# Spectral mixer with gMLP gate: w_in tail rows loaded as four 32-row transfers, and a reordered start of the chunk schedule

## The chip, the cores and the metric

The kernel runs on one core of one Trainium2 chip. The metric is the device time in microseconds of one execution. The engines are named as the profile names them: PE (TensorE, matrix products), PEld (its weight loads), DVE (VectorE), ACT (ScalarE), POOL (GpSimd) and SP (SyncE, which only issues DMA transfers here). "SPq", "ACTq" and "POOLq" are the issue of transfers on those queues.

## The reference

The input x is 2048 rows of 576 values in bf16. After a layer norm, the result goes two ways, and both are joined at the end.

```
xn = layernorm(A_x)                                  # (1, 2048, 576)

# branch A: a filter in the frequency domain
X  = rfft2(xn); X = X * (w_r + 1j * w_i)             # (2048, 289) complex
s  = irfft2(X)                                       # (2048, 576)

# branch B: a gated MLP with a product over the sequence
z  = gelu(xn @ w_in)                                 # w_in: (576, 4608)
z1 = z[..., :2304];  z2 = layernorm(z[..., 2304:])
g  = einsum('ts,bsf->btf', w_sp, z2) + b_sp          # w_sp: (2048, 2048)
b  = (z1 * g) @ w_out                                # w_out: (2304, 576)

return A_x + s * silu(b)
```

The inputs A_x, w_r, w_i, w_in, w_sp, b_sp and w_out are bf16. B_x is not used.

## The kernel before, in words

The 2048 rows are 16 tiles of 128 rows, counted by m. Four tiles of x are one group in SBUF (`XC[0]` to `XC[3]`).

**Start and row DFT.** For each tile m, `ln1` takes the row statistics on DVE (two L259 instructions and L260), and the reciprocal root comes from ACT (L263) for m below 2 and from POOL (L248, L250) for the others. `ln1_apply` (L276, L279) writes the normalised tile to one of three buffers. It splits the 576 columns into two halves of 288, each with 256 main columns and 32 "tail" columns, so a tile has five blocks of 128: four main ones and one that holds both halves' tails, twice. `xpose` (L287) transposes the five blocks on PE into one PSUM buffer, and ACT copies them to `xnT` (L288). `p0_fold` (L294, L295, DVE) forms sums and differences of the halves, and `p0` (L302, six products of 290 columns) is the DFT along a row, with the constants CDSD. ACT copies it out (L304), and POOL stores it to DRAM (L306).

**Chunks.** The product with w_in is cut into 168 chunks: 96 "z2" chunks (one row tile by 384 columns, L410) and 72 "z1" chunks (128 columns by 512 rows, L495). A chunk has four products over 128 rows of w_in and one over the 64 tail rows (two halves of 32). The tail rows lie twice in SBUF, in partitions 0 to 63 and 64 to 127, so that two tail products of different chunks run beside each other. `fill(n)` emits the next n chunks in the order of the string `kinds`; with every fourth chunk it emits the tails of four chunks, of which two are held open in PSUM. ACT applies gelu (L429, L423, L504). For z2, DVE takes statistics (L437) and normalises in place (L466). These DVE steps are queued, and each chunk emits up to `pace` of them. The chunks are put between the steps of the DFT as filling, so that PE has work while the DFT waits.

**Order.** SP, PE and DVE run in the order in which the program is written. The order on ACT and POOL is set by the scheduler. The stages are: the loop over m with row DFTs and chunks; eleven chunks; `p1` (L320), the first column DFT; twelve chunks; `p2` and `p3` (L344, L356), the second column DFT, the filter and its inverse; twelve chunks; `p4` (L370) and `p5` (L385), the inverse transforms, whose result is stored as Yd; the remaining chunks; then the product with w_sp (`main`, L558) and the output product (`outm`, L612). Between the DFT stages the data go through DRAM and back. The transposed blocks of w_sp ("slabs") are loaded by L476, and `slab_sums` (L481) forms sums of them, because the 2x2 block product is done with seven block products instead of eight.

**Loads.** All loads of the start are on SP's queue, in this order: tiles 0 and 1 of x, CDSD, tiles 2 and 3, then three times the group of four transfers of `load_win` for 768 columns of w_in followed by four tiles of x (L223), then constants G1 (L244). `load_win` has two transfers for the main rows (L231) and two for the tails (L233); each of the two tail transfers reads 2 x 32 rows and fills 64 partitions:

```
for r in range(2):
    nc.sync.dma_start(out=t[r * KT:(r + 1) * KT, KS - 1, :], in_=wv[:, 2 * P:H2, fs])
```

Here `wv` is w_in seen as two halves, so the source is [2, 32, columns]. The same function later loads six groups of 384 columns for the z1 chunks.

PSUM has two pools of buffers: "h" with four buffers, for transposes and chunks, and "a" with two, for the DFT steps. At the very start, PE runs ten products on zeros (L673), and two more after the first transpose (L677).

Of the kernel before, what the change touches and what calls it, by code (L numbers as in the profile page):

```python
# [14 lines left out]
P = 128  # L15
# [71 lines left out]
def kernel(  # L87
# [59 lines left out]
    nc.scalar.dma_start(out=ident[:], in_=cd_id.ap())  # L147
# [66 lines left out]

    def load_x(c):
        t = AIN[c][:, 0:4 * D].rearrange("p (m d) -> p m d", m=4)
        if c == 0:
            for i in range(4):
                nc.sync.dma_start(out=t[:, i, :], in_=xv[:, i, :])
                if i == 1:  # L220
                    nc.sync.dma_start(out=CDSD, in_=cd_cdsd.ap().rearrange("p (a k l) -> p a k l", a=2, k=3))
        else:
            nc.sync.dma_start(out=t, in_=xv[:, 4 * c:4 * c + 4, :])  # L223
        return t
# [4 lines left out]
    def load_win(t, fs):  # L229
        for a in range(2):  # L230
            nc.sync.dma_start(out=t[:, a:KS - 1:2, :], in_=wv[a, 0:2 * P, fs].rearrange("(b p) f -> p b f", p=P))  # L231
        for r in range(2):
            nc.sync.dma_start(out=t[r * KT:(r + 1) * KT, KS - 1, :], in_=wv[:, 2 * P:H2, fs])  # L233
# [6 lines left out]
    XC = [load_x(0)]  # L240
    for g in range(3):
        load_win(WIN2[:, :, 2 * g * ZC:2 * (g + 1) * ZC], slice(Fh + 2 * g * ZC, Fh + 2 * (g + 1) * ZC))
        XC.append(load_x(g + 1))
# [9 lines left out]
    def ln1(ms):  # L253
        n = len(ms)
        mv = small.tile([P, n, 2], F32, tag=f"mv{n}", bufs=5)
        for i, m in enumerate(ms):
            st = small.tile([P, 2, 6], F32, tag="st1", bufs=4)
            for h in range(2):
                nc.vector.bn_stats(out=st[:, h, :], in_=XC[m // 4][:, m % 4, h * H2:(h + 1) * H2])  # L259
            nc.vector.bn_aggr(out=mv[:, i, :], in_=st[:])  # L260
        if ms[0] < 2:
            rs = small.tile([P, n], F32, tag=f"l1{n}r", bufs=5)
            nc.scalar.activation(out=rs[:], in_=mv[:, :, 1], func=ACT.Sqrt, bias=eps[:], scale=1.0)  # L263
            nc.vector.reciprocal(out=rs[:], in_=rs[:])
        else:
            rs = rstd_of(mv, n, f"l1{n}")
        for i, m in enumerate(ms):
            ln1_of[m] = (mv[:, i, 0:1], rs[:, i:i + 1])

    ln1_of = {}  # L270
# [200 lines left out]
    SA = dict(P1=4, P2=1, P5=2, P4=3, P6=0, P7=5, P3=6)  # L471
# [6 lines left out]
    def slab_sums(i, it):  # L478
        for o, a, b, op in ((5, 4, 2, ALU.subtract), (2, 2, 3, ALU.add), (0, 2, 4, ALU.subtract), (6, 1, 0, ALU.subtract)):
# [152 lines left out]
    kinds = "2" * (MT + 12) + "2221" * 4 + "2" * 12 + "12112111" * 6 + "21" * 12 + "2212" * 3 + "22112221"  # L632
# [11 lines left out]
    def fill(n, pace=1):  # L644
        for _ in range(n):
# [5 lines left out]
            if i % 4 == 1:  # L651
                done = held[:]
# [16 lines left out]
    with tc.manual_schedule(engines={SP, PE, DVE}):  # L669
# [9 lines left out]
        ln1([0])  # L679
        ln1_apply(0)  # L680
        xpose(0)
        keep_warm(2)
        ln1([1])
        ln1_apply(1)
        nc.scalar.activation(out=THF[:, 0:1], in_=ln1_of[1][0], func=ACT.Gelu_apprx_tanh)
        p0_fold(0)
        xpose(1)
        ln1([2])
        p0(0)
        fill(1, 0)  # L690
        ln1_apply(2)
        p0_fold(1)
        fill(1, 0)
        xpose(2)
        p0(1)
        ln1([3])
        ln1_apply(3)
        fill(1, 0)
        nc.sync.dma_start(out=MM, in_=cd_mm.ap().rearrange("p (a k) -> p a k", a=3))
        ln1([4])  # L700
        for m in range(2, MT):
# [3 lines left out]
            if m + 3 < MT:  # L705
                ln1([m + 3])
# [3 lines left out]
            p0(m)  # L710
            if m in (6, 9):
# [5 lines left out]
        for s2 in range(0, N2, 2):  # L717
            p1(s2)
            fill(1)
# [17 lines left out]
        for u in range(4 * NLC):  # L737
            p4(u)
            fill(1)
# [6 lines left out]
        rest = kinds.rindex("2") + 1 - place[0]  # L746
        for i in range(NT // P):
            fill(rest // 4, 2)
            slab_sums(i, 0)
# [54 lines left out]
```

## Time and profile before

| | before |
|---|---|
| median of 11 runs | 519.28 us (516.62 to 524.11) |
| profiled execution: time, span | 519.93 us, 518.1 us |
| PE busy, share of the span | 503.6 us, 97% |
| DVE, ACT, POOL busy | 332.8, 171.6, 208.1 us |
| mean granted clock of PE | 0.986 |
| HBM read, written | 40.55 MB, 21.26 MB |
| chunks done when the loop over m ends (51.28 us) | 17 of 168 |

The span runs from the first to the last instruction; the time of the execution is 1.8 us longer. The profile cuts the span into 40 slices (of 13 us), and gives for each the busy share in tenths, the clock that PE was granted, and how busy the 16 DMA engines were. Stretches of any length can be asked for in the same way. A line of the timeline gives start, length, engine, source line, operation, and in brackets the idle time before it and what ended it. Line numbers are those of the kernel before; the changed kernel's own lines differ by a few.

### The profile page before, as it was taken

What the parts mean: (1) busy time and instruction counts of PE and PEld (TensorE: products, weight loads), DVE (VectorE), ACT (ScalarE), POOL (GpSimd) and SP (SyncE); (2) the same over time, 40 slices, a digit from 0 to 9 for tenths busy, and PEclk for the clock granted to TensorE, in tenths of its full rate; (3) what the DMA queues carried; (4) which work ended last, traced back from release to release, by engine and by line L of the source; (5) the groups of instructions that cost most, each with busy time, mean ns of one, the idle gap of its engine ahead of it and who ended that gap; (6) DMA issues with size and microseconds to landing.
All of it is one profiled execution on the core that took longest, in us unless ns stands there. A gap on an engine that the chain in (4) does not pass through costs nothing.

```text
span 518.1 us, 9262 instructions
## 1 busy us (share of the span) xinstructions
PE 503.6 (97%) x3454; PEld 316.6 (61%) x3454; DVE 332.8 (64%) x712; ACT 171.6 (33%) x356; POOL 208.1 (40%) x285
## 2 busy tenths in 40 slices
PE   6979999999999999999999999999999999999996
PEld 2546554444546664356666577666666678888885
DVE  5676989655536484956656656766666637777734
ACT  4666878656557857520000001100000011000001
POOL 2455133523332486854344411344434301555500
PEclk9798999999999999999999999999999999999999
DMA  8673768887566696464021269412111655111302
GB/s 252 175 245 103 241 224 254 276 260 231 166 194 232 136 242 173 142 193 147 31 62 32 62 128 211 131 43 61 31 51 42 148 103 149 33 42 42 86 17 77
DMA packets 85409, 70.81 MB, mean 137 GB/s; under 512 B 39220, under 2 KB 77876, under 8 KB 85108
## 3 DMA queue, kind: packets, MB, share of 16 engines
q1 hardware_dynamic: 80068, 56.08, 40.6%
q0 software_dynamic: 5152, 14.11, 8.3%
q8 instruction: 27, 0.44, 0.4%
q14 instruction: 18, 0.15, 0.1%
q10 hardware_dynamic: 144, 0.03, 0.0%
HBM read 40.55 MB, written 21.26 MB: 119 GB/s over the span
## 4 chain that ended last, share of the span: by engine, by line
PE 86%; SPq 6%; DMA 5%; DVE 1%; issue 1%; ACT 1%; POOL 0%; DVEq 0%; POOLq 0%
PE pm L558 42%; PE ph L495 14%; PE ph L410 13%; PE po L612 9%; DMA AR<-in_A_x_dram 3%; SPq L476 2%; PE pa L385 2%; PE pb L356 2%; SPq L233 1%; PE pa L370 1%; DMA AR<-c_cdsd 1%; PE pa L320 1%; PE pa L302 1%; PE pa L344 1%; PE pl L612 1%; SPq L231 1%
## 5 line engine op out<-in xcount | busy, mean ns | idle before, releaser
L558 PE MATMUL pm<-AR,Z 128*128 128x384 bf16 (+1 forms) x864 | 138.8, 308 | 0.0
L562 DVE TENSOR_TENSOR AR<-pm,AR 128x384 f32<-128x384 f32 (+3 forms) x162 | 82.1, 512 | 71.8 <-PE pm L558 39.7
L558 PEld LDWEIGHTS <-Z 128*128 128x128 bf16 x864 | 84.5, 98 | 40.6
L558 PE MATMUL pm<-AR 128*128 128x384 bf16 (+1 forms) x648 | 107.0, 308 | 1.2 <-DVE AR L481 0.9
L410 PE MATMUL ph<-AR 128*128 128x384 bf16 (+1 forms) x480 | 92.5, 334 | 3.4 <-DMA AR<-in_B_w_in_dram 3.2
L495 PE MATMUL ph<-AR 128*128 128x512 bf16 (+1 forms) x360 | 85.2, 379 | 0.0
L558 PEld LDWEIGHTS <-AR 128*128 128x128 bf16 x648 | 63.3, 98 | 33.5 <-issue 3.2
L572 ACT ACTIVATE AR<-pm 128x384 f32<-128x384 f32 (+1 forms) x27 | 12.3, 454 | 188.0 <-PE pm L558 188.0
L546 POOL TENSOR_TENSOR AR<-Z,AR 128x1024 bf16<-128x1024 bf16 x27 | 57.8, 2142 | 34.7 <-PE pm L558 32.8
L612 PE MATMUL po<-AR 128*128 128x288 bf16 x540 | 66.6, 286 | 0.0
L410 PEld LDWEIGHTS <-AR 128*128 128x128 bf16 (+1 forms) x480 | 40.8, 99 | 41.2 <-issue 22.4
L612 PEld LDWEIGHTS <-AR 128*128 128x128 bf16 x594 | 56.9, 98 | 13.9
L515 POOL DMA_DIRECT2D Z1d<-AR x58 | 32.9, 568 | 65.4 <-ACT AR L504 60.9
L573 POOL TENSOR_TENSOR AR<-AR 128x384 f32<-128x384 f32 (+1 forms) x27 | 22.8, 843 | 76.7 <-ACT AR L572 76.7
L504 ACT ACTIVATE AR<-ph 128x512 bf16<-128x512 f32 x72 | 42.5, 596 | 16.9 <-PE ph L495 14.1
L495 PEld LDWEIGHTS <-AR 128*128 128x128 bf16 (+1 forms) x360 | 30.5, 97 | 28.5 <-issue 4.6
L437 DVE BATCH_NORM_STATS2 st<-Z 128x6 f32<-128x384 bf16 x66 | 33.7, 547 | 18.3 <-ACT Z L429 18.3
L429 ACT ACTIVATE Z<-ph 128x384 bf16<-128x384 f32 x66 | 30.9, 492 | 24.2 <-PE ph L410 23.9
L615 ACT ACTIVATE TH<-po 128x576 f32<-128x576 f32 x15 | 9.8, 650 | 78.0 <-PE po L612 74.2
L569 DVE TENSOR_TENSOR AR<-AR 128x384 bf16<-128x384 bf16 (+1 forms) x108 | 31.7, 334 | 0.9
L346 DVE TENSOR_TENSOR AR<-pa,AR 128x578 bf16<-128x578 f32 x32 | 22.7, 750 | 13.6 <-PE pa L344 13.6
L616 DVE SCALAR_TENSOR_TENSOR AR<-TH,po 128x576 bf16<-128x576 f32 x15 | 11.3, 751 | 30.1 <-ACT TH L615 30.1
(76 smaller groups left out, 487.8 us busy)
## 6 DMA issues: line engine op xcount, KB each, us to landing
Z1d<-AR POOLq DMA_DIRECT2D x58, 128.0 KB, 3.9
AR<-Z1d SPq DMA_DIRECT2D x36, 192.0 KB
AR<-in_A_x_dram SPq DMA_DIRECT2D x20, 144.0 KB
AR<-in_B_w_out_dram SPq DMA_DIRECT2D x1, 2592.0 KB
Ad<-AR POOLq DMA_DIRECT2D x16, 144.5 KB, 5.6
AR<-Ad SPq DMA_DIRECT2D x4, 578.0 KB
AR<-in_A_w_r_dram SPq DMA_DIRECT2D x16, 144.5 KB
AR<-in_A_w_i_dram SPq DMA_DIRECT2D x16, 144.5 KB
```

Of the source, the lines that this page charges most:

```text
L410: nc.tensor.matmul(self.ph[:], lhsT=xnT[rows, self.m, ks, :], rhs=WIN2[rows, ks, n * ZC:(n + 1) * ZC], start=start, stop=stop)
L429: nc.scalar.activation(out=zc, in_=ph[:], func=ACT.Gelu_apprx_tanh)
L437: nc.vector.bn_stats(out=z2s[m][:, n, :], in_=zc)
L495: nc.tensor.matmul(self.ph[:].rearrange("p (a t) -> p a t", a=4), lhsT=wb[rows, ks, (fi % WG) * P:(fi % WG + 1) * P], rhs=xnT[rows, 4 * tq ...
L504: nc.scalar.activation(out=zs, in_=ph[:], func=ACT.Gelu_apprx_tanh)
L515: (nc.sync if place[0] > len(kinds) - 16 else nc.gpsimd).dma_start(out=d, in_=s_)
L546: nc.gpsimd.tensor_tensor(out=t, in0=zblk(p, 1, 0), in1=t2, op=ALU.subtract)
L558: nc.tensor.matmul(dst, lhsT=z[:, s, :], rhs=SLB[SA[name]][:, s, 0:nt], start=(s == 0 and not more), stop=(s == HM - 1), skip_group_check= ...
L562: nc.vector.tensor_tensor(out=out, in0=x, in1=y, op=ALU.add)
L569: nc.vector.tensor_tensor(out=o, in0=o, in1=zb[:, f, h, 0:nt], op=ALU.mult)
L573: nc.gpsimd.tensor_tensor(out=p1a, in0=p1, in1=B[0], op=ALU.add)
L612: nc.tensor.matmul(pv[:, hh, :], lhsT=U[:, fi, h, i * P:(i + 1) * P], rhs=WOUT[:, fi, c0 + hh * H2:c0 + hh * H2 + w // nh], start=(fi == 0 ...
```

## The change

The transfer of the tails is cut into four of 32 rows, each with a source [32, columns] and a target of 32 partitions. The first loads change their order and partly their queue. In the start, two z2 chunks follow the first transpose, and the folds and the row DFT of tile 0 come after them. The loop over m emits one chunk more for m = 2 and 3 and for each odd m from 5 (the start and loop together emit 26 chunks instead of 17). Two chunks fewer are emitted in each of the stages `p1` and `p4`, five fewer at the end of the filling, and `kinds` is rewritten to go with it. The reciprocal root of tile 1 comes from POOL. The sums of the slabs are formed in another order and placed in other buffers, and in the first round they come in two parts. The diff:

```diff
@@ -144,7 +144,6 @@
     ident = pers.tile([P, P], BF16)
     TH = pers.tile([P, 2, D], F32)
     cd_id = nc.inline_tensor(_bf16_np(np.eye(P)), name="c_id")
-    nc.scalar.dma_start(out=ident[:], in_=cd_id.ap())
     eps = pers.tile([P, 1], F32)
     nc.vector.memset(eps[:], 1e-5)
     mhalf = pers.tile([P, 1], F32)
@@ -212,35 +211,36 @@
     warm = Z2[:, MT - 1, 0:512]
     nc.vector.memset(warm, 0.0)
 
+    XC = [AIN[c][:, 0:4 * D].rearrange("p (m d) -> p m d", m=4) for c in range(4)]
+
     def load_x(c):
...
+        nc.sync.dma_start(out=XC[c], in_=xv[:, 4 * c:4 * c + 4, :])
 
     HT = H2 - 2 * P
     wv = B_w_in.rearrange("(a d) f -> a d f", a=2)
 
-    def load_win(t, fs):
+    def load_win(t, fs, after_main=None):
         for a in range(2):
             nc.sync.dma_start(out=t[:, a:KS - 1:2, :], in_=wv[a, 0:2 * P, fs].rearrange("(b p) f -> p b f", p=P))
-        for r in range(2):
-            nc.sync.dma_start(out=t[r * KT:(r + 1) * KT, KS - 1, :], in_=wv[:, 2 * P:H2, fs])
+        if after_main:
+            after_main()
+        for q in range(4):
+            nc.sync.dma_start(out=t[q * HT:(q + 1) * HT, KS - 1, :], in_=wv[q % 2, 2 * P:H2, fs])
 
     def load_win1(g):
         fs = slice((g % (FT // WG)) * WG * P, (g % (FT // WG) + 1) * WG * P)
         wb = WIN1[g % 2]
         load_win(wb, fs)
 
-    XC = [load_x(0)]
+    nc.scalar.dma_start(out=XC[0][:, 0, :], in_=xv[:, 0, :])
+    nc.scalar.dma_start(out=ident[:], in_=cd_id.ap())
+    nc.sync.dma_start(out=XC[0][:, 1, :], in_=xv[:, 1, :])
     for g in range(3):
-        load_win(WIN2[:, :, 2 * g * ZC:2 * (g + 1) * ZC], slice(Fh + 2 * g * ZC, Fh + 2 * (g + 1) * ZC))
-        XC.append(load_x(g + 1))
+        load_win(WIN2[:, :, 2 * g * ZC:2 * (g + 1) * ZC], slice(Fh + 2 * g * ZC, Fh + 2 * (g + 1) * ZC),
+                 None if g else lambda: nc.sync.dma_start(out=XC[0][:, 2:4, :], in_=xv[:, 2:4, :]))
+        if g == 0:
+            nc.sync.dma_start(out=CDSD, in_=cd_cdsd.ap().rearrange("p (a k l) -> p a k l", a=2, k=3))
+        load_x(g + 1)
     nc.sync.dma_start(out=G1, in_=cd_g1.ap().rearrange("p (s k) -> p s k", s=N2))
 
     def rstd_of(mv, n, tag):
@@ -250,23 +250,27 @@
         nc.gpsimd.tensor_tensor(out=rs[:], in0=ve[:], in1=mhalf[:, 0:n], op=ALU.pow)
         return rs
 
...
+    def ln1_stats(m, hs=(0, 1)):
+        if hs[0] == 0:
+            st1[m] = small.tile([P, 2, 6], F32, tag="st1", bufs=4, name="st1")
+        for h in hs:
+            nc.vector.bn_stats(out=st1[m][:, h, :], in_=XC[m // 4][:, m % 4, h * H2:(h + 1) * H2])
+
+    def ln1_aggr(m):
+        mv = small.tile([P, 1, 2], F32, tag="mv1", bufs=5, name="mv1")
+        nc.vector.bn_aggr(out=mv[:, 0, :], in_=st1[m][:])
+        if m == 0:
+            rs = small.tile([P, 1], F32, tag="l11r", bufs=5, name="rs1")
             nc.scalar.activation(out=rs[:], in_=mv[:, :, 1], func=ACT.Sqrt, bias=eps[:], scale=1.0)
-            nc.vector.reciprocal(out=rs[:], in_=rs[:])
         else:
-            rs = rstd_of(mv, n, f"l1{n}")
-        for i, m in enumerate(ms):
-            ln1_of[m] = (mv[:, i, 0:1], rs[:, i:i + 1])
-
+            rs = rstd_of(mv, 1, "l11")
+        ln1_of[m] = (mv[:, 0, 0:1], rs[:, 0:1])
+
+    def ln1(m):
+        ln1_stats(m)
+        ln1_aggr(m)
+
+    st1 = {}
     ln1_of = {}
 
     def ln1_apply(m):
@@ -468,15 +472,16 @@
 
     wspv = B_w_sp.rearrange("t (b p) -> t b p", p=P)
 
-    SA = dict(P1=4, P2=1, P5=2, P4=3, P6=0, P7=5, P3=6)
+    SA = dict(P1=4, P2=1, P5=0, P4=3, P6=5, P7=2, P3=6)
     RAW = (4, 1, 2, 3)
 
     def load_slab(it, a, i):
         r0 = a // 2 * (S // 2) + ITS[it][0] + i * P
         nc.sync.dma_start_transpose(out=SLB[RAW[a]][:, :, i * P:(i + 1) * P], in_=wspv[r0:r0 + P, a % 2 * HM:(a % 2 + 1) * HM, :])
 
-    def slab_sums(i, it):
-        for o, a, b, op in ((5, 4, 2, ALU.subtract), (2, 2, 3, ALU.add), (0, 2, 4, ALU.subtract), (6, 1, 0, ALU.subtract)):
+    def slab_sums(i, it, part=None):
+        ops = ((0, 2, 3, ALU.add), (2, 4, 2, ALU.subtract), (5, 0, 4, ALU.subtract), (6, 1, 5, ALU.subtract))
+        for o, a, b, op in ops if part is None else ops[:2] if part == 0 else ops[2:]:
             sl = slice(i * P, (i + 1) * P)
             (nc.gpsimd if o == 6 and it == 0 else nc.vector).tensor_tensor(out=SLB[o][:, :, sl], in0=SLB[a][:, :, sl], in1=SLB[b][:, :, sl], op=op)
 
@@ -629,7 +634,7 @@
     zq = iter(range(MT * NZC))
     yq = iter(range(FT * 4))
     tick = [0]
-    kinds = "2" * (MT + 12) + "2221" * 4 + "2" * 12 + "12112111" * 6 + "21" * 12 + "2212" * 3 + "22112221"
+    kinds = "2" * 37 + "2221" * 3 + "2" * 14 + "12112111" * 6 + "21" * 11 + "2212" * 3 + "2221"
     kinds += "2" * (MT * NZC - kinds.count("2")) + "1" * (FT * 4 - kinds.count("1"))
     held = []
     place = [0]
@@ -641,7 +646,7 @@
         for ks in range(KS - 1):
             c.mm(ks, slice(0, P), first and ks == 0, not first and ks == KS - 2)
 
-    def fill(n, pace=1):
+    def fill(n, pace=1, before_tails=None):
         for _ in range(n):
             i = place[0]
             place[0] += 1
@@ -649,6 +654,8 @@
                 held.append(chunk(i))
                 full(held[-1], True)
             if i % 4 == 1:
+                if before_tails:
+                    before_tails()
                 done = held[:]
                 held[:] = [chunk(i + 1), chunk(i + 2)]
                 for r, c in enumerate(sorted(done + held, key=lambda c: c.wide)):
@@ -676,38 +683,46 @@
             for i in range(n):
                 nc.tensor.matmul(pw[:], lhsT=warm[:, 0:P], rhs=warm, start=True, stop=True)
 
-        ln1([0])
+        ln1(0)
+        ln1_stats(1, (0,))
+        nc.vector.reciprocal(out=ln1_of[0][1], in_=ln1_of[0][1])
         ln1_apply(0)
+        nc.scalar.activation(out=THF[:, 0:1], in_=ln1_of[0][1], func=ACT.Gelu_apprx_tanh)
         xpose(0)
+        ln1_stats(1, (1,))
+        ln1_aggr(1)
         keep_warm(2)
-        ln1([1])
+        fill(1, 0)
+        ln1(2)
         ln1_apply(1)
-        nc.scalar.activation(out=THF[:, 0:1], in_=ln1_of[1][0], func=ACT.Gelu_apprx_tanh)
         p0_fold(0)
-        xpose(1)
-        ln1([2])
-        p0(0)
-        fill(1, 0)
         ln1_apply(2)
+
+        def first_p0():
+            xpose(1)
+            p0(0)
+
+        fill(1, 0, first_p0)
+        ln1(3)
         p0_fold(1)
-        fill(1, 0)
         xpose(2)
+        fill(2, 0)
+        ln1_apply(3)
+        ln1(4)
         p0(1)
-        ln1([3])
-        ln1_apply(3)
-        fill(1, 0)
         nc.sync.dma_start(out=MM, in_=cd_mm.ap().rearrange("p (a k) -> p a k", a=3))
-        ln1([4])
         for m in range(2, MT):
             if m + 1 < MT:
                 xpose(m + 1)
             p0_fold(m)
             if m + 3 < MT:
-                ln1([m + 3])
+                ln1(m + 3)
             if m + 2 < MT:
                 ln1_apply(m + 2)
             fill(1, 0)
             p0(m)
+            if m < 4 or m % 2:
+                fill(1, 0)
             if m in (6, 9):
                 load_win1(m // 9)
         for ch in range(4):
@@ -716,7 +731,8 @@
         fill(11, 2)
         for s2 in range(0, N2, 2):
             p1(s2)
-            fill(1)
+            if s2 % 16 != 14:
+                fill(1)
             if s2 == N2 // 2:
                 load_w(1)
         for ch in range(4):
@@ -736,19 +752,22 @@
         fill(12, 2)
         for u in range(4 * NLC):
             p4(u)
-            fill(1)
+            if u % 6 != 5:
+                fill(1)
         for j in range(MT):
             p5(j)
             if j < 4 * NT // P:
                 load_slab(0, (0, 2, 1, 3)[j % 4], j // 4)
             fill(1)
         load_z1(0)
-        rest = kinds.rindex("2") + 1 - place[0]
+        fill(kinds.rindex("2") + 1 - place[0], 2)
         for i in range(NT // P):
-            fill(rest // 4, 2)
-            slab_sums(i, 0)
-        fill(rest - 3 * (rest // 4), 3)
+            fill(2, 3)
+            slab_sums(i, 0, 0)
         nc.sync.dma_start(out=BB, in_=B_b_sp.rearrange("(a s) -> a s", a=1).to_broadcast((P, S)))
+        for i in range(NT // P):
+            fill(2, 3)
+            slab_sums(i, 0, 1)
         fill(len(kinds) - place[0], 3)
         z1_store(None, None)
         assert not stats_q and not norm_q
```

## The prediction

> **What bounds the kernel now.** I read the page from the top: shares, then slices, then stretches of the first 60 us, then the timeline of TensorE there.
>
> ```profile
> PE 503.6 (97%) x3454; PEld 316.6 (61%) x3454; DVE 332.8 (64%) x712; ACT 171.6 (33%) x356; POOL 208.1 (40%) x285
> ...
> PE   6979999999999999999999999999999999999996
> ...
> PEclk9798999999999999999999999999999999999999
> ```
>
> TensorE is busy 97% of the span. Its digits fall below 9, and its clock below 9 tenths, only in the first slices and at the end. A saved stall must therefore lie in the first 52 us, or be paid for by TensorE work removed. This change removes no matmul: 96 z2 and 72 z1 chunks stay. The stretches (columns: PE, PEld, DVE, ACT, POOL busy; clock; DMA share; GB/s) show two holes:
>
> ```profile
> 12.00:14.00 2.00, 0.02 (x3) 0.01 (x2) 0.80 (x3) 0.49 (x1) 0.73 (x2) 0.64 0.73 209
> 14.00:16.00 2.00, 2.00 (x12) 1.11 (x12) 0.20 (x1) 1.02 (x2) 0.00 (x0) 0.50 0.46 107
> ...
> 34.00:36.00 2.00, 0.41 (x4) 0.10 (x1) 0.00 (x0) 1.31 (x3) 0.00 (x0) 1.00 0.28 85
> 36.50:37.50 1.00, 0.00 (x0) 0.00 (x0) 0.97 (x5) 0.00 (x0) 0.23 (x1) 0.50 0.12 49
> ```
>
> In both, TensorE stands still and the DMA share falls: at 36.5 us to 0.12, two engines' worth of 16, at 49 GB/s. After each hole the clock is 0.50 (until about 19.3 and 43.3 us). The timeline names the waits:
>
> ```profile
> 9.41 1.30 PE L410 MATMUL ph<-AR 128*128 128x384 bf16 x7 [0.24 <-DMA AR<-in_B_w_in_dram]
> 11.69 0.32 PE L410 MATMUL ph<-AR 64*128 64x384 bf16 x1 [0.99 <-DMA AR<-in_B_w_in_dram]
> 13.99 0.79 PE L410 MATMUL ph<-AR 64*128 64x384 bf16 x3 [1.98 <-DMA AR<-in_B_w_in_dram]
> ...
> 36.12 0.82 DVE L259 BATCH_NORM_STATS2 st<-AR 128x6 f32<-128x288 bf16 x2 [3.40 <-DMA AR<-in_A_x_dram]
> ```
>
> The main w_in rows are there at 9.41, the first tail at 11.69, the second 2.30 us later. The last x load, issued at 21.24, lands at 36.12. From 51.12 on TensorE runs gapless.
>
> **What the Trainium skill says.** "DMA: Bandwidth & Descriptors", section "Why a DMA increments its semaphore by 16 and not by 1": a transfer is split over the largest number of engines, up to 16, that divides the slowest dimension of both sides. The old tail's source is [2, 32, 768], so two engines; the trace agrees (share 0.12, and 98,304 B / 2 / 2.30 us = 21.4 GB/s per engine). The new source and target start with 32 rows, so 16; no run here shows that yet. Same page, "Queues, rings and completion order": one engine takes its descriptors in ring order. So x rows queued behind tails wait for the two crowded engines; the 36.12 landing agrees. "TensorE: Matmul & The Clock Gate", "Part 1": an idle window of about 3.4 us halves the clock; both holes above agree.
>
> **Two checks of the model on before.** On each crowded engine lie 37 KB of x0 to x3, 28 of CDSD, and three times (49 main + 98 tails + 37 x): 617 KB. At 21.4 GB/s that is 28.8 us; with the start at 2.1 us and ten row-DFT stores (9 KB each per engine, 4.3 us) it gives 35.2, measured 36.1. Early on the whole stream is slower: 1.82 MB by 9.41, so 249 GB/s from 2.1 us.
>
> **The change, part by part.**
>
> *Tails.* Four of 32 rows put 12 KB on every engine instead of 98 KB on two. Up to the last x load each engine then carries 362 KB: 16.9 us at 21.4 GB/s, or for 5.8 MB at 249 GB/s 23.3. With the start and six to eight stores it lands at 22 to 29 us. Nine groups gain two SP issues each (old issue 0.56 us), +18; the order of the built program shows each SP transfer waiting for the one eight earlier, but then over 1 MB is still under way, so this is hidden by the transfers themselves. Uncovered: at most 6 x 0.5 = 3 us in the start.
>
> *Order of loads.* x0 and ident go to ACT's queue, ahead of its table load (1.28 us), which is needed at 4.19 and has 1.4 us left: zero. If it were not covered, under 0.9 us. CDSD moves behind the mains, x2-3 (now one issue) and tails: 2.05 MB ahead of it at 249 GB/s, so 10.3 us. The gelu table load moves from 6.98 to about 4.5, under the first transposes, and ends with its dummy about when the transposes end (6.0); lost cover would cost 1.5 us.
>
> *First steps.* Chunk 0 starts when ACT has copied the first transpose, 6.85 (before: 8.85), chunk 1 follows, done at 8.2. DVE now has tile 2's statistics ahead of apply(1), behind it fold(0): x2-3 arrives at 1.41 MB, 7.8 us; 0.82+0.21 statistics, 0.65 apply, so transpose 1 at 9.4 and row DFT 0 at 10.4, done 11.2; four tails, 11.5. The next transpose needs a PSUM buffer that the gelu of chunk 0 frees, and ACT does the DFT copy (0.82) first: 12.5. Then transpose 0.28, chunks 2 and 3 at 0.65, DFT(1) 0.75: the loop over m=2.. starts at 14.9. Tile 4 (2.64 MB, 12.7 us) is just in time.
>
> *The loop.* It holds 14 transposes (0.28) and DFTs (0.75), and now 22 chunks. Eleven chunks took 8.92 us from 51.12, so 0.81 each with tails. TensorE: 14 x 1.03 + 22 x 0.81 = 32.2 us, 2.30 per m. DVE needs 1.97 per m (0.82+0.21 statistics, 0.65 apply, two folds 0.49, overlapped starts), ACT about 2.0. Before, the good stretch ran at 2.04 against DVE's 1.97, so I add 0.1 per m: 33.6. End of loop 48.5, with 26 chunks done; before it was 51.28 with 17. No x or w_in load is then late: m=9 comes at about 31.7.
>
> *Later stages.* Nine chunks fewer remain: 9 x 0.81 = 7.3 us. They are taken out of the loop's tail, after s2=14 and 30 (L320 stage), after u=5 and 11 (L370 stage) and from the end. Without a chunk there, u=6 follows u=5 after 0.45 us and waits for DVE's 1.22 us copy of u=4: about 0.3 us each, 0.6 together. The time from the last L320 product to the first L344 one shrinks from 10.2 to 9.4 us; the write was issued at 78.06 and the first read at 80.99, and with some 3 us more for its landing this still fits before 86.4: zero, at worst 1 us. DVE's statistics after the loop are the same 21 ahead of its first L324 copy (10.4 us), and have one chunk more of cover; the passes queued behind them fill 14.3 of 16.2 us. Slab sums: same twelve in the first round, those that wait for the Yd stores (4.3 us on DVE before) now last and covered by 18 z1 chunks instead of 14. In later rounds the first sum needs the last loaded slab; the loads were issued by 324.92, the sums ran from 329.89: zero, at worst 0.7.
>
> *Sum.* (51.28 - 48.5) + 7.3 - 0.6 = 9.5 us. Against the profiled run (519.93, its span 518.1) that is 510.4; the median of 11 runs is 0.65 lower, so **509.8 us**.
>
> Unknown: whether the clock falls between 8 and 14 us. Before, TensorE was busy some 35% of 9 to 14 us and lost it; now about 60%. I take no fall; one would cost some 3 us (6 us at half clock), two 6 us. The other end is a loop without overhead and an earlier start: 46.2 for its end, 12.4 us saved, and some 2 us more if loads run at the later 300 GB/s and above.
>
> **Rivals.**
> 1. *ACT and the four PSUM buffers become the bound.* For: ACT was busy 8.64 of 10 us at 20 to 30, and gains half a gelu per m. Against: its operations overlap at issue. At 2.7 us per m the loop ends at 52.7: -1.4 + 7.3 - 0.6 = 5.3, so 514.
> 2. *The tails stay narrow* (the spread does not happen). x still lands at 36.1, the loop ends near 53.3: 5 us saved by the moved chunks, 514.5. Against: the stated rule.
> 3. *Slower: small transfers cost a fixed time in series.* If each tail held its queue 2.3 us whatever its width, 12 tails instead of 6 push the last x load by 13.8 us to 49.9; then come the 15.2 us that followed it before and about 2 us of added chunks, 67.1: -15.8 + 7.3 = 8.5 slower, 528. It decides from about 1.3 us per tail, where that x load lands past 41. Against: the share of 0.12 says that the other engines were idle, not that issue was slow. The SP order, with its wait for the transfer eight back, speaks for some of it.
>
> **How the numbers follow.** 0.72 for the forecast, 0.15 for rivals 1 and 2, 0.05 for a gain swallowed by clock and stalls, 0.08 for the third. Half a per cent, 2.6 us, is about what a measurement can tell from no change: faster 0.87, same 0.05, slower 0.08. The range is 504.5 (best loop, fast loads) to 516 (two clock falls of 3 us).
>
> **What would show it.** Right: tail waits at L414 gone or under 0.5 us; no stretch in the first 40 us with a DMA share of 0.12; the last x tile's statistics not waiting; gapless TensorE from about 15 us; first L320 product near 57.5 us instead of 60.15, with 9 chunks more already done. Wrong: clock 0.5 after 10 us, ACT waits for TensorE gone while TensorE waits for ACT each m, or a DMA wait on x beyond 30 us.

## The result, and the profile after

The changed kernel takes 514.7 us (median of 13 runs, 512.33 to 520.78) against 519.03 us for the kernel before (median of 51): the ratio is 0.9922, with an interval of 0.9904 to 0.9939. The ratio leaves out the run of 520.78 us, which was in a slow state, and is not the plain quotient of the two medians. The kernel is faster, as forecast, but by some 4 us and not by 9.5. The two profiled executions lie further apart, 513.53 against 519.93 us (spans 511.6 and 518.1), because the profiled one of before is 0.9 us above its median and that of after 1.2 us below its own. So about 2 us of the 6.4 between them is the draw of the two executions.

The page of the changed kernel, its shares and two rows of slices:

```profile
PE 499.5 (98%) x3454; PEld 314.8 (62%) x3454; DVE 332.2 (65%) x711; ACT 170.8 (33%) x355; POOL 207.6 (41%) x284
...
PE   7999998999999999999999999999999999999996
...
PEclk9999999999999999999999999999999999999999
```

The number of matmuls is the same, 3454. After the first slice, the early dips in both rows are gone. One digit is below 9 that was not before: the seventh slice, 77 to 90 us, which held 9 in the kernel before. Everything below comes back to it.

The stretches of the changed kernel at the places of the two old holes (PE, PEld, DVE, ACT, POOL busy; clock; DMA share; GB/s):

```profile
12.00:14.00 2.00, 2.00 (x18) 1.37 (x17) 1.28 (x6) 1.70 (x4) 1.70 (x3) 1.00 1.08 286
14.00:16.00 2.00, 2.00 (x19) 1.51 (x18) 1.93 (x8) 1.52 (x3) 0.87 (x2) 1.00 1.08 365
...
34.00:36.00 2.00, 2.00 (x20) 1.07 (x18) 1.97 (x9) 1.74 (x4) 1.70 (x4) 1.00 0.37 112
36.00:38.00 2.00, 2.00 (x20) 1.48 (x18) 1.26 (x6) 1.77 (x4) 1.55 (x4) 1.00 0.13 44
```

Both holes are filled: TensorE is busy all the time at full clock, and the DMA engines move 286 to 365 GB/s at 12 to 16 us, where it was 209 and 107. The share of 0.13 at 36 us means something else than the 0.12 did before: the loads are over, and nobody waits for them. A DMA share alone doesn't tell a starved kernel from one that has all its data; the TensorE column beside it does.

What TensorE waits for in the whole span (us in total, times, longest), first the two longest entries of the kernel before, then three of the changed kernel:

```profile
PE pt L287 <- DVE AR L276: 4.5, 3, 3.1
PE ph L410 <- DMA AR<-in_B_w_in_dram: 3.2, 3, 2.0
```

```profile
PE pb L360 <- DVE AR L350: 2.0, 1, 2.0
PE pt L291 <- ACT Z L433: 1.6, 3, 0.8
...
PE ph L414 <- ACT AR L292: 0.7, 2, 0.6
```

The waits for w_in (L410 in the old numbers) are gone, and a new one heads the list: one wait of 2.0 us at `p3` (L360) for a DVE sum (L350). In the changed kernel's lines, `p0` is L306, `p1` L324, `p2` L348, `p3` L360, the product with w_sp L563, a z2 chunk L414 and a z1 chunk L500.

To see where the start's gain went, I follow the stages (start or end of TensorE's work there, us), and correct for the chunks that one kernel has done earlier: 0.81 us for a z2 chunk, 1.04 for a z1 chunk. The sum is the lead of after over before.

| point | before | after | time saved | chunks ahead, worth | lead |
|---|---|---|---|---|---|
| end of the loop over m (last L306 product) | 51.28 | 46.68 | 4.6 | 6.5 | 11.1 |
| first `p1` product | 60.15 | 56.34 | 3.8 | 7.3 | 11.1 |
| end of `p1` | 77.05 | 73.05 | 4.0 | 6.5 | 10.5 |
| first `p2` product | 87.23 | 82.39 | 4.8 | 5.4 | 10.3 |
| end of `p3` | 146.16 | 144.43 | 1.7 | 5.4 | 7.2 |
| end of `p5` | 198.19 | 195.13 | 3.1 | 3.4 | 6.4 |
| first product with w_sp | 221.33 | 215.23 | 6.1 | 0 | 6.1 |

The lead at the end of the loop is better than forecast. Most of what is lost later, 3.1 of 5.0 us, goes between the first `p2` product and the end of `p3`. It goes there all at once: the lead is 2.96 us at 87.90, 1.44 at 91.54, and then stays between 1.4 and 1.7 us to the end of `p3` (these three are in time alone). The timeline of TensorE in the changed kernel shows the place:

```profile
82.39 0.41 PE L348 MATMUL pa<-AR 128*128 128x289 bf16 x2
...
85.54 0.38 PE L500 MATMUL ph<-AR 64*128 64x512 bf16 x2
87.90 1.13 PE L360 MATMUL pb<-AR 128*128 128x289 bf16 x4 [1.98 <-DVE AR L350]
88.82 1.91 PE L500 MATMUL ph<-AR 128*128 128x512 bf16 x4
```

The first `p2` product ends at 82.80. TensorE then has three chunks and another `p2` product to do, and at 85.92 it has nothing left. The sum that it needs starts on DVE only at 86.44. The same four products of L360 and L500 then take 1.13 and 1.91 us, where 0.67 and 1.02 are usual: the clock has fallen. The stretches give it in the column before the last two:

```profile
84.00:86.00 2.00, 1.92 (x12) 0.79 (x11) 1.97 (x7) 0.57 (x2) 0.00 (x0) 1.00 1.19 317
86.00:88.00 2.00, 0.10 (x1) 0.10 (x1) 2.00 (x5) 0.71 (x2) 1.55 (x4) 0.96 1.06 408
88.00:90.00 2.00, 2.00 (x7) 0.91 (x7) 2.00 (x4) 0.65 (x1) 1.67 (x6) 0.50 0.97 386
90.00:92.00 2.00, 2.00 (x9) 0.99 (x8) 1.97 (x4) 0.86 (x2) 0.40 (x2) 0.69 0.72 189
```

DVE is busy for 1.97 to 2.00 of 2 us in all four: it is the engine that is late. What it does instead of the sum is in its timeline in the changed kernel:

```profile
83.03 0.88 DVE L470 TENSOR_SCALAR Z<-Z,mv,rs 128x2304 bf16<-128x2304 bf16 x1 [0.44 <-POOL rs L250]
83.94 0.76 DVE L470 TENSOR_TENSOR Z<-Z 128x1152 bf16<-128x1152 bf16 x1
84.61 1.01 DVE L441 BATCH_NORM_STATS2 st<-Z 128x6 f32<-128x384 bf16 x2
85.66 0.32 DVE L457 BATCH_NORM_AGGREGATE mv<-st 128x2 f32<-128x36 f32 x1
...
85.97 0.55 DVE L441 BATCH_NORM_STATS2 st<-Z 128x6 f32<-128x384 bf16 x1
86.44 1.41 DVE L350 TENSOR_TENSOR AR<-pa,AR 128x578 bf16<-128x578 f32 x2
```

The operand of the sum is ready at 82.80, but the sum starts 3.6 us later. Apart from the first 0.2 us, in which DVE waits for POOL (L250), that time goes to z2 statistics (L441, L457) and normalising (L470), which stand ahead of the sum in DVE's order. The kernel before has the same sum (L346 there) and the same kind of work ahead of it, with its operand ready at 87.64:

```profile
88.17 1.01 DVE L437 BATCH_NORM_STATS2 st<-Z 128x6 f32<-128x384 bf16 x2
89.21 0.32 DVE L453 BATCH_NORM_AGGREGATE mv<-st 128x2 f32<-128x36 f32 x1
89.45 1.36 DVE L346 TENSOR_TENSOR AR<-pa,AR 128x578 bf16<-128x578 f32 x2
```

There it is 1.8 us late, and the chunks cover that without a gap.

Where the extra DVE work comes from can be counted in the program itself, since it is written out in order. The chunks in the loop over m are emitted with `pace` 0: they put steps into the statistics queue and take none out. So the chunks moved into the loop leave a longer queue behind:

| statistics queue | before | after |
|---|---|---|
| steps waiting at the start of the eleven chunks (after the first of them) | 19 | 28 |
| steps waiting in the twelve chunks before `p2` (after the first of them) | 8 | 18 |
| steps emitted in these twelve chunks, at up to two each | 20 | 24 |
| steps still waiting after them | 2 | 9 |

Before, the queue ran down to two steps, and the twelve chunks found only 20 to emit. After, it never runs dry, every chunk emits its two, and DVE gets four steps more. At the same time the stretch is one chunk shorter for TensorE, since no chunk follows the last `p1` product. From the start of the last copy out of `p1` to the sum DVE takes 13.35 us (73.09 to 86.44), against 12.36 before (77.09 to 89.45); TensorE takes 9.34 us from the end of `p1` to the first `p2` product, against 10.18. The two differences, 1.0 and 0.8 us, make up the 1.8 us by which the sum is later against its operand than before (3.6 against 1.8).

### The profile page after: what moved, and what is told of

It is laid out like the page before. It is cut to its first block, busy times and chain, and to the rows that moved or that the text cites. A ratio compares the mean times of both kernels' runs of the same rounds, so it can differ in the third digit from the quotient of the medians.

```text
span 511.6 us, 9283 instructions
## 1 busy us (share of the span) xinstructions
PE 499.5 (98%) x3454; PEld 314.8 (62%) x3454; DVE 332.2 (65%) x711; ACT 170.8 (33%) x355; POOL 207.6 (41%) x284
## 4 chain that ended last, share of the span: by engine, by line
PE 84%; DVE 5%; ACT 3%; SPq 3%; DMA 2%; issue 2%; POOL 1%; DVEq 0%; POOLq 0%; ACTq 0%
PE pm L563 42%; PE ph L500 13%; PE ph L414 11%; PE po L617 8%; SPq L480 2%; PE pa L306 2%; PE pa L389 2%; PE pb L360 2%; DMA AR<-in_A_x_dram 1%; PE pa L374 1%; PE pl L617 1%; ACT Z L427 1%; DVE st L441 1%; PE pt L291 1%; DMA AR<-Yd 1%
## 5 line engine op out<-in xcount | busy, mean ns | idle before, releaser
L563 PE MATMUL pm<-AR,Z 128*128 128x384 bf16 (+1 forms) x864 | 138.8, 308 | 0.0
L563 PEld LDWEIGHTS <-Z 128*128 128x128 bf16 x864 | 84.5, 98 | 40.6
L563 PE MATMUL pm<-AR 128*128 128x384 bf16 (+1 forms) x648 | 107.0, 308 | 1.1 <-DVE AR L486 0.6
L414 PE MATMUL ph<-AR 128*128 128x384 bf16 (+1 forms) x480 | 88.7, 328 | 0.9 <-ACT AR L292 0.7
L500 PE MATMUL ph<-AR 128*128 128x512 bf16 (+1 forms) x360 | 84.1, 382 | 0.0
L563 PEld LDWEIGHTS <-AR 128*128 128x128 bf16 x648 | 63.3, 98 | 33.2 <-issue 3.0
L551 POOL TENSOR_TENSOR AR<-Z,AR 128x1024 bf16<-128x1024 bf16 x27 | 57.8, 2142 | 33.4 <-PE pm L563 33.4
L414 PEld LDWEIGHTS <-AR 128*128 128x128 bf16 (+1 forms) x480 | 39.8, 97 | 34.5 <-issue 14.4
L520 POOL DMA_DIRECT2D Z1d<-AR x55 | 31.4, 572 | 59.9 <-ACT AR L509 58.7
L578 POOL TENSOR_TENSOR AR<-AR 128x384 f32<-128x384 f32 (+1 forms) x27 | 23.2, 860 | 76.9 <-ACT AR L577 76.9
L500 PEld LDWEIGHTS <-AR 128*128 128x128 bf16 (+1 forms) x360 | 30.1, 98 | 33.0 <-issue 9.2
L441 DVE BATCH_NORM_STATS2 st<-Z 128x6 f32<-128x384 bf16 x66 | 33.5, 545 | 5.0 <-ACT Z L433 5.0
L350 DVE TENSOR_TENSOR AR<-pa,AR 128x578 bf16<-128x578 f32 x32 | 22.7, 752 | 15.0 <-PE pa L348 15.0
L621 DVE SCALAR_TENSOR_TENSOR AR<-TH,po 128x576 bf16<-128x576 f32 x15 | 11.3, 753 | 30.1 <-ACT TH L620 30.1
```

The source lines that it names most:

```text
L414: nc.tensor.matmul(self.ph[:], lhsT=xnT[rows, self.m, ks, :], rhs=WIN2[rows, ks, n * ZC:(n + 1) * ZC], start=start, stop=stop)
L441: nc.vector.bn_stats(out=z2s[m][:, n, :], in_=zc)
L500: nc.tensor.matmul(self.ph[:].rearrange("p (a t) -> p a t", a=4), lhsT=wb[rows, ks, (fi % WG) * P:(fi % WG + 1) * P], rhs=xnT[rows, 4 * tq ...
L520: (nc.sync if place[0] > len(kinds) - 16 else nc.gpsimd).dma_start(out=d, in_=s_)
L551: nc.gpsimd.tensor_tensor(out=t, in0=zblk(p, 1, 0), in1=t2, op=ALU.subtract)
L563: nc.tensor.matmul(dst, lhsT=z[:, s, :], rhs=SLB[SA[name]][:, s, 0:nt], start=(s == 0 and not more), stop=(s == HM - 1), skip_group_check= ...
```

## The experiments

All ratios are to the kernel before, run in the same batch on the same chip (517.98 us in the first batch of four, 518.22 in the second). The letters in the expectations are theirs; each says there what it claims. Short names: tails only, tails undone, and so on, after the labels.

**1. Tails only.** The kernel before with nothing but the four 32-row transfers:

```diff
-        for r in range(2):
-            nc.sync.dma_start(out=t[r * KT:(r + 1) * KT, KS - 1, :], in_=wv[:, 2 * P:H2, fs])
+        for q in range(4):
+            nc.sync.dma_start(out=t[q * HT:(q + 1) * HT, KS - 1, :], in_=wv[q % 2, 2 * P:H2, fs])
```

> The kernel before with the four 32-row tail transfers and nothing else. Theory A (the two crowded DMA engines made both holes of the start): tail waits and the x wait at 36 us go, the share of 0.12 goes, the clock stays at 1.0, the loop over m runs at about 2.04 us per tile (DVE) and ends near 44 us instead of 51.3; the first wait of the L356 line is not longer than before, since DVE's queue has the same content; total 511 to 513 us. Rival (the gain came from the moved chunks and the new order of the start): the holes shrink by less than 2 us together and the total stays above 516.

Measured: 510.53 us, ratio 0.9857 (0.9828 to 0.9886). This one edit alone is worth 7.4 us, more than the whole change, and a little more than expected. Its waits of TensorE, and the two stretches of the holes:

```profile
PE pt L287 <- DVE AR L276: 1.9, 3, 1.0
...
PE ph L410 <- DMA AR<-in_B_w_in_dram: 0.7, 1, 0.7
```

```profile
12.00:14.00 2.00, 1.82 (x18) 1.40 (x18) 1.01 (x5) 1.81 (x4) 0.73 (x2) 1.00 1.09 365
36.00:38.00 2.00, 2.00 (x18) 1.38 (x18) 1.27 (x6) 1.46 (x4) 1.31 (x3) 1.00 0.23 74
```

The wait for w_in is 0.7 us once. The loop ends at 41.86 with the old 17 chunks, 9.42 us earlier than before, and this lead stays: 9.41 at the first `p1` product, at the first `p2` product, at the end of `p3` and at the first product with w_sp. Nothing is given back, because the statistics queue is that of before: the sum is 1.8 us late (78.23 to 80.03) and covered.

**2. Tails undone.** The changed kernel with the two narrow transfers back (the diff of experiment 1 reversed).

> The changed kernel with the old two 64-partition tail transfers. Theory A: x and w_in come late again, the loop ends near 52 us instead of 46.7, the clock falls to 0.5 once or twice, total 519 to 521 us. Rival (order and moved chunks carry the gain): total at most 516 us.

Measured: 517.47 us, ratio 1.0004 (0.9982 to 1.0026). That is less than the 519 to 521 us expected, but without the wide tails the change is worth nothing. TensorE's longest wait in this kernel, and its stretch at 12 us:

```profile
PE pa L306 <- DMA AR<-c_cdsd: 4.7, 1, 4.7
```

```profile
12.00:14.00 2.00, 0.00 (x0) 0.00 (x0) 0.67 (x3) 0.00 (x0) 0.63 (x2) 0.50 0.57 160
```

In the new order of loads CDSD stands behind the tails. Narrow, they hold it up, the first row DFT starts at 14.25 instead of 9.71 us, and the clock is at half. The wait of 2.0 us at L360 is there as well (`p3` starts at 93.76), so it has nothing to do with the loads.

**3. Fewer statistics.** The changed kernel, one step per chunk in the twelve chunks before `p2` instead of two:

```diff
-        fill(12, 2)
+        fill(12, 1)
         p2(0)
```

> The changed kernel with one DVE step of the statistics queue per chunk instead of two in the twelve chunks between the L324 and the L348 stage. Theory B (in the changed kernel DVE is about 3.6 us behind when the first L350 product is due, TensorE waits 2.0 us for it at L360 and then runs some 3 us at half clock): the wait is gone, the clock stays 1.0 there, the lag of the first two L348/L360 pairs goes, total 511 to 512 us (3 less than the changed kernel). Rival (the round trip through DRAM or the larger number of SP transfers holds that stage): the wait moves to a DMA or stays, total within 1 us of the changed kernel.

Measured: 510.77 us, ratio 0.9855 (0.9833 to 0.9877), apart from the interval of after. The timeline of this kernel, first TensorE and then DVE:

```profile
82.17 0.41 PE L348 MATMUL pa<-AR 128*128 128x289 bf16 x2
...
85.63 0.67 PE L360 MATMUL pb<-AR 128*128 128x289 bf16 x4
```

```profile
79.96 0.88 DVE L470 TENSOR_SCALAR Z<-Z,mv,rs 128x2304 bf16<-128x2304 bf16 x1 [0.89 <-POOL rs L250]
82.62 1.43 DVE L350 TENSOR_TENSOR AR<-pa,AR 128x578 bf16<-128x578 f32 x2 [1.78 <-PE pa L348]
```

Now DVE waits for TensorE and not the other way round: the sum starts 0.04 us after its operand, L360 has no wait, and the clock is 1.00 from 84 to 94 us. The lead is 11.1 us after `p3` (after: 7.2) and 10.0 at the first product with w_sp. The postponed steps are done later, in the pairs of `p2` and `p3`, and disturb nothing there. So the queue of statistics ahead of one sum is the cause of most of what was given back.

**4. Old counts.** The changed kernel with its loads, start and slab sums, but the chunk counts and `kinds` of before:

```diff
-    kinds = "2" * 37 + "2221" * 3 + "2" * 14 + "12112111" * 6 + "21" * 11 + "2212" * 3 + "2221"
+    kinds = "2" * (MT + 12) + "2221" * 4 + "2" * 12 + "12112111" * 6 + "21" * 12 + "2212" * 3 + "22112221"
...
-            if m < 4 or m % 2:
-                fill(1, 0)
...
-            if s2 % 16 != 14:
-                fill(1)
+            fill(1)
...
-            if u % 6 != 5:
-                fill(1)
+            fill(1)
```

> The changed kernel with the old number of chunks in the loop over m (no second chunk) and after the L324 and L374 stages, and the old order string. Loads and first steps stay changed. Theory A and B: the loop is bound by DVE at 2.0 us per tile and ends near 43 to 44 us, the stage from L324 to L360 looks as in the kernel before (no wait of TensorE for L350), total 510 to 512 us. Rival (the moved chunks carry the gain): total 515 us or more.

Measured: 513.93 us, ratio 0.9907 (0.9885 to 0.9929), so slower than expected. The part that was meant came out: `p3` follows `p2` at 82.40 after 78.88 with no wait (20 steps in the twelve chunks, as before), and the first product with w_sp is at 212.05, about where tails only has it (211.92). But then a wait appears that none of the theories had. TensorE's timeline in this kernel, and DVE's ahead of it:

```profile
218.11 1.47 PE L563 MATMUL pm<-AR 128*128 128x384 bf16 x8 [2.00 <-DVE AR L567]
```

```profile
209.49 2.60 DVE L547 TENSOR_TENSOR AR<-Z 128x1024 bf16<-128x1024 bf16 x1
212.12 2.50 DVE L549 TENSOR_TENSOR AR<-AR,Z 128x1024 bf16<-128x1024 bf16 x1
217.50 0.56 DVE L567 TENSOR_TENSOR AR<-pm,AR 128x384 f32<-128x384 f32 x1 [2.88 <-POOL AR L578]
```

POOL has three slab sums in a row (7.51 us from 206.56), late against the first products with w_sp, and L551 and L578 on POOL come after them. POOL begins these three only 5.5 us ahead of the first product with w_sp here, but 10.8 us ahead in the changed kernel (from 204.42) and 8.6 in the kernel before (from 212.72). So the old counts and the new sums don't fit each other, and this run doesn't isolate the counts.

**5. `p1` chunks back.** The changed kernel with a chunk after each `p1` step again, to give TensorE its missing cover (two chunks more there, two fewer at the end, with `kinds` to match):

```diff
-            if s2 % 16 != 14:
-                fill(1)
+            fill(1)
```

> The changed kernel with a chunk again after every L324 step (two more there, two fewer at the end). Theory B1 (the length of DVE's queue before the first L350 product decides, not the one missing chunk of cover): TensorE gets 0.84 us more before L348 and DVE one step more, so the wait at L360 falls only from 2.0 to about 1.6 us, the clock still falls there, total 514 to 515 us. Theory B2 (the missing cover is the cause): the wait falls below 0.5 us, total 511 to 512.5 us.

Measured: 511.96 us, ratio 0.9886 (0.9854 to 0.9918). Its timeline at `p3`, and the stretch after:

```profile
89.33 0.67 PE L360 MATMUL pb<-AR 128*128 128x289 bf16 x4 [1.96 <-DVE AR L350]
```

```profile
88.00:90.00 2.00, 0.67 (x5) 0.50 (x6) 2.00 (x3) 0.00 (x1) 1.80 (x4) 1.00 0.96 398
```

The wait is unchanged, 1.96 us, and so is the lag of the sum (84.15 to 87.87, 3.7 us): the twelve chunks still emit 24 steps from a queue of 16. Giving the chunk back does not shorten the wait; a shorter queue does (experiment 3). So the wait is nearer to theory B1 (1.6 us) than to B2 (below 0.5), but the total is in the range of B2: the clock stayed at 1.00 here. For each run the mean granted clock is known: of the six runs of this kernel, the four at 0.998 or above took 510.87 to 512.06 us, the two at 0.995 and 0.997 took 513.80 and 513.97. In the changed kernel only four of the 13 runs are at 0.999 or above, and these took 512.33 to 514.24. So the same wait costs the clock in some executions and not in others. It was rarer in this sample; that the restored chunks made it so is not shown, and the last section gives a reason why it need not be theirs.

**6. Fewer statistics, `p4` chunks back.** Experiment 3 with a chunk after each `p4` step again (`kinds` with `"21" * 12`), for what goes around `p4` and `p5` (0.8 us in the table above):

```diff
-        fill(12, 2)
+        fill(12, 1)
         p2(0)
...
-            if u % 6 != 5:
-                fill(1)
+            fill(1)
```

> The changed kernel with one DVE step per chunk between L324 and L348 (as in e3) and a chunk again after every L374 step. Theory: beside the 3 to 4 us of e3, the 0.7 us that TensorE lost around L374 and L389 come back; total 510 us, at best 0.7 below e3. Rival: nothing was lost there, total as e3.

Measured: 510.48 us, ratio 0.9848 (0.9821 to 0.9875). The interval holds that of experiment 3 almost wholly, and the spans are 508.5 and 508.7: the two cannot be told apart, so this loss is too small to be settled here.

**7. Old start.** The changed kernel with the old order of the first loads, the old first steps and the reciprocal root of tile 1 from ACT; the wide tails and the second chunks in the loop over m are kept. The old start holds one chunk fewer:

```diff
-    nc.scalar.dma_start(out=XC[0][:, 0, :], in_=xv[:, 0, :])
-    nc.scalar.dma_start(out=ident[:], in_=cd_id.ap())
-    nc.sync.dma_start(out=XC[0][:, 1, :], in_=xv[:, 1, :])
...
+    for i in range(4):
+        nc.sync.dma_start(out=XC[0][:, i, :], in_=xv[:, i, :])
...
-        fill(1, 0, first_p0)
...
+        xpose(1)
+        ln1(2)
+        p0(0)
+        fill(1, 0)
```

> The changed kernel with the old order of the first loads (on SP, CDSD after two tiles) and the old order of the first steps; tails, chunk counts and everything later stay changed (one chunk fewer is done when the loop ends, since the old start holds three). Theory C (the new start order is worth next to nothing once the tails are wide, for DVE and the arrival of the loads pace the first tiles): loop end within 1 us of 46.7, wait of 2 us at L360 as in the changed kernel, total 514 to 516 us. Rival (the two chunks after the first transpose are worth their 2 us): loop ends near 49, total near 517 us.

Measured: 515.16 us, ratio 0.9942 (0.9923 to 0.9962), overlapping that of after. The loop ends at 46.36 us, with the new start at 46.68; with the missing chunk (0.81 us) counted, the new start is 0.5 us ahead. With wide tails the order of the first steps decides nothing more that these runs can tell, and the comparison is not a clean one: the wait at `p3` (L359 here) is 3.0 us instead of 2.0, and the clock falls again:

```profile
89.03 1.13 PE L359 MATMUL pb<-AR 128*128 128x289 bf16 x4 [3.01 <-DVE AR L349]
```

**8. Warm in the wait.** The changed kernel with seven products on zeros ahead of the first `p3` product, which keep TensorE busy while it waits but do no work:

```diff
             fill(1)
+            if hh == 0:
+                keep_warm(7)
             p3(hh)
```

> The changed kernel with seven products on zeros (1.5 us at full clock) put on TensorE just ahead of the first L360 step, where it stands still for 2 us. Their result is not used. Theory B (2 us of waiting and then some 3 us at half clock): the first L360 still begins near 87.9, the clock stays 1.0 after it, total 1 to 1.5 us less than the changed kernel. Rival (the half clock costs nothing, since DVE paces that stage): total unchanged.

Measured: 512.21 us, ratio 0.9888 (0.9861 to 0.9915). Its timeline, and the stretch after the wait:

```profile
86.99 1.67 PE L684 MATMUL pw<-Z 128*128 128x512 bf16 x7 [0.36 <-ACT Z L433]
88.62 0.66 PE L360 MATMUL pb<-AR 128*128 128x289 bf16 x4
```

```profile
88.00:90.00 2.00, 2.00 (x13) 1.00 (x11) 2.00 (x4) 0.65 (x1) 1.58 (x6) 1.00 1.00 410
```

`p3` begins no earlier, but its four products take 0.66 us and not 1.13. Four of the five runs have a mean clock of 1.000 and the fifth 0.998. From after to experiment 3 (0.9922 to 0.9855) the gain is 0.67% or 3.5 us, and the intervals lie apart. The ratio here, 0.9888, lies halfway, but its interval overlaps both others, so these runs don't split the 3.5 us between the clock and the wait. An estimate from the trace bounds the clock's part: in the changed kernel the half clock lasts 3.41 us (87.84 to 91.25), which costs at most 1.7 us of TensorE's work, and only in the executions that have it.

## Why the prediction was partly right

Point by point, in its own steps.

- **What bounds the kernel.** Right. The two holes were the tails' doing: one edit closes both (experiment 1), and without it the rest gains nothing (experiment 2).
- **Tails.** Right. The Trainium skill, "DMA: Bandwidth & Descriptors", "Why a DMA increments its semaphore by 16 and not by 1", says that the slowest dimension sets the number of engines; the prediction noted that no run showed this for 32 rows. Now the traces agree: 365 GB/s and a DMA share of 1.09 at 12 to 14 us in experiment 1, where the kernel before had 209 GB/s and a share of 0.73, and then 107 and 0.46. The edit makes the transfers wider and smaller at once, and no run has one without the other. In the changed kernel no statistics wait for x after 7.89 us. The price that was set for more issues, at most 3 us, did not appear: the four tail issues of the first group take 1.92 us on SP's queue, hidden by the transfers.
- **First steps.** Close. Chunk 0 starts at 7.37 us (forecast 6.85), the second transpose at 9.29 (9.4), the first tails are done at 11.07 (11.5) and the loop starts at 14.21 (14.9). That the clock would not fall between 8 and 14 us was right. The clock fell in none of the traces with wide tails before 80 us. What the new start is worth beside them is small: 0.5 us of lead in experiment 7, and nothing that the ratios can tell.
- **The loop.** Right in price. 14.21 to 46.68 is 32.5 us with 21 chunks and, with the one that follows directly, 33.3 against the forecast of 33.6. The lead at its end is 11.1 us, where the forecast's own numbers give (51.28 − 48.5) + 9 × 0.81 = 10.1.
- **Later stages.** This is the step that failed. Its 7.3 us for nine chunks fewer holds only if the other engines keep up with the shorter stages. The prediction looked at DVE's queue for the stage of `p1` ("the same 21 ahead of its first L324 copy"; "The passes queued behind them fill 14.3 of 16.2 us") and stopped there. For the time up to the first L344 product it looked at the DMA alone ("zero, at worst 1 us"). That time came out as forecast, 9.34 us against 9.4. But for DVE's sum after that product (L346, in the changed kernel L350) it had no term at all, so the stage of `p2` and `p3` was put at nothing without a reason. A chunk moved into the loop takes its statistics along only into the queue, not through DVE. The ten steps more of backlog kept the queue full in the twelve chunks just ahead of `p2`, and the sum of L350 waited behind them. That cost 3.1 us in the profiled pair, 3.5 us in the ratios, for a forecast of nothing.
- **The same step, its small terms.** Forecast 0.6 us lost for the missing chunks after u=5 and 11 and none for those after s2=14 and 30. Measured 0.6 in `p1` and, from the end of `p3` to the end of `p5`, 0.8. From there to the first product with w_sp the lead falls by another 0.3 us without a wait of TensorE; whether the first slab sums are behind it is not shown. For the sums of the later rounds (forecast zero, at worst 0.7) TensorE waits 0.6 us in the changed kernel and 0.9 in the kernel before. In experiment 3, which reaches that point 3.9 us earlier, it waits 1.2 us.
- **The clock.** The forecast took no fall and allowed for one of about 3 us, but between 8 and 14 us. It came at 88 us, after a wait that the forecast did not have. The prediction also says that both holes agree with an idle window of about 3.4 us. They don't: TensorE stood still for 0.99 and then 1.98 us in the first and for 3.12 us in the second, and the clock fell all the same. The last section shows what the traces give instead.
- **The rivals.** ACT as the bound: a trace of it, 1.6 us in three waits at L291, not 2.7 us per m. Tails that stay narrow: did not happen. A fixed time per small transfer: did not happen, twelve of them pass under the stream. The measured 514.7 lies near the number of the first two, but for neither's reason.

So in the profiled pair: 11.1 us of lead at the end of the loop, less 0.8 from the start of `p1` to the start of `p2`, less 3.1 at the first `p2` and `p3`, less 1.1 from the end of `p3` to the first product with w_sp, plus 0.4 in what follows, is the 6.5 us between the spans. Against the medians the gain is smaller by another 2 us, which is the draw of the profiled executions.

The best versions are experiments 6, 1 and 3, at 510.48, 510.53 and 510.77 us, with intervals that overlap. Tails alone is the simplest. The moved chunks and the new start bring 1.7 us or more of lead at the end of the loop (11.1 or 11.3 against 9.4), of which experiment 3 still has 0.6 at the first product with w_sp and nothing at the end.

What stays open: how the 3.5 us divide between the wait and the clock; the losses of 0.6 us in `p1` and 0.8 us around `p4` and `p5`; and the slab sums, which no run isolates from the chunk counts.

## What to carry to other kernels

Before filler work is moved to an earlier place, list what each piece leaves for the other engines, and carry that queue forward, step by step, to the next instruction on that engine that the critical one waits for: a cover that was checked for one stage says nothing of the next. A transfer that keeps two of sixteen DMA engines busy costs most through what is queued behind it, so look at the landing of the next load and not at its own duration. And try the smallest edit of a large change alone: here it was worth more than the whole.

## What the runs showed of the hardware

- **The clock falls after about half an idle window, so the same standstill can end either way.** The Trainium skill, "TensorE: Matmul & The Clock Gate", "Part 1", gives about 3.4 us of idling for a fall, with a window that runs freely. In the ten traces here the granted clock changes only at times that lie whole multiples of 3.41 us apart within a trace, so that each execution can be cut into such windows. At full clock, six windows had TensorE idle for 1.78 us or more, by its busy time as the profile models it: 1.78 and 2.05 in the kernel before, 1.92 in the changed one, 2.42, 2.00 and 3.01 in experiments 2, 4 and 7. Half clock followed each. Some 1450 had 1.75 us or less, and it followed none (1.75 was at the standstill of experiment 2, whose 1.99 us are split between two windows). At half clock, three windows with 1.07 us idle or more kept it there, and six with 0.49 or less ended it. That is about half an idle window where the page has a whole one, and the measurement decides. The place of the windows differs from execution to execution. In the changed kernel, 1.92 of the 1.98 us of standstill lie in one window; in experiment 5 the 1.96 us are split into 1.08 and 0.88 (two windows of each kernel; the number after the comma is TensorE's busy time, the column before the last two the clock):

```profile
84.43:87.84 3.41, 1.49 (x10) 0.48 (x8) 3.38 (x10) 0.98 (x2) 1.39 (x4) 1.00 1.12 368
87.84:91.25 3.41, 3.35 (x11) 1.55 (x11) 3.38 (x7) 1.13 (x2) 1.89 (x6) 0.50 0.87 302
```

```profile
85.03:88.44 3.41, 2.34 (x14) 0.92 (x14) 3.38 (x9) 2.06 (x4) 1.45 (x6) 1.00 1.14 346
88.44:91.85 3.41, 2.52 (x16) 1.21 (x16) 3.38 (x6) 0.69 (x2) 2.20 (x4) 1.00 0.95 370
```

If the window starts at random, an estimate from these figures (1.78 of 3.41 us must fall into one window) is that a standstill of 1.98 us costs the clock in some 54% of the executions. The runs fit: a mean clock below 0.998 is found in nine of the 13 of the changed kernel and in two of the six of experiment 5, and in none of the five with products on zeros in the wait (experiment 8). A mean doesn't tell where the clock fell.

- **x0 on ACT's queue came later.** Its first statistics start at 3.82 us in the changed kernel, 0.7 us later than from SP's queue in the kernel before (3.09). The other first loads changed too, so that the queue is the reason is not shown. Chunk 0 comes 0.5 us later than forecast.
- **DVE and POOL hold each other up.** In experiment 4 the DVE operations L547 and L549 take 2.60 and 2.50 us beside POOL's sums of 2.50 us each; in the kernel before (L542, L544), which start with no POOL sum running, 0.69 us each. The Trainium skill, "SBUF — State Buffer", "Who interferes with whom", says that a DVE operation with two SBUF inputs and a GpSimd operation that reads SBUF exclude each other for a whole instruction; the durations agree.
